# Attention and two MoE layers on one core: a deeper weight decode, tanh gates, and stacked fp32r scores

## The chip, the core and the metric

The kernel runs on one core of one Trainium2 chip. Its engines work side by side, each through its own queue in order: TensorE (PE, with its weight loads as PEld), VectorE (DVE), ScalarE (ACT), GpSimd (POOL), and SyncE (SP), which here only issues DMAs. The metric is the device time of one execution in microseconds. A profiled execution also has a span, from the first to the last recorded instruction; the times inside a profile count from the span's start.

## The reference

Attention over 4 batches, 8 heads, 576 positions and 64 dimensions keeps, in each row of scores, the 32 largest; then come two MoE layers with dense weights (512 to 1536 and back) over the 2304 tokens.

```python
scores = scale * np.matmul(q, k.transpose(0, 1, 3, 2))
kth = np.partition(scores, -top_k, axis=-1)[..., -top_k:-top_k + 1]
scores = np.where(scores >= kth, scores, -1000000000.0)
attn = np.exp(scores - np.max(scores, axis=-1, keepdims=True))
attn = attn / (np.sum(attn, axis=-1, keepdims=True) + 1e-09)
x = np.matmul(attn, v)                       # heads joined: (2304, 512)
g = x @ w_gate
x = (g * (1.0 / (1.0 + np.exp(-g))) * (x @ w_val)) @ w_out      # first MoE
gate = 1.0 / (1.0 + np.exp(-(x @ w2_gate)))
out = (gate * (x @ w2_val)) @ w2_out                            # second MoE
```

The weights come to the core as 64-bit floats and are turned into fp32 on it.

## The kernel before

The tokens are cut into six chunks of 4, 5, 6, 7, 7 and 7 query tiles of 64 tokens (`SIZES`). For each chunk `attention` computes x, head pair by head pair, and `moe` runs both MoE layers on it. A segment is the part of a chunk that lies in one batch, for one head pair.

Scores: `score_ops` multiplies a tile of 64 queries by 288 keys, one head at a time. Two query tiles and two heads are four matmuls on different quarters of the array (64 rows by 64 columns, fp32), which fill one PSUM tile `ps_s`; ACT copies it to `s` (`cp`). A row tile is 128 rows of 576 scores. `row_tile` finds its 32nd largest score on DVE with four MAX8 and three MATCH_REPLACE8 steps, ACT takes exp of all scores into `e`, and DVE masks and sums them in one operation (`mask`, L695). The reciprocal of the sum scales the row, `turned` transposes it on PE into `ps_t`, and `pv` multiplies it by V into `ps_v`.

Weights: a slab is 1024 columns of 128 rows; it has two half-slabs. Chunk 0 runs with plain fp32 weights (mode N), and `decode` makes them: a DMA brings a half-slab of 64-bit numbers (`wr`), ACT scales the high words to `wf`, the sign and the lower bits are brought to `wu`, and DVE merges both (L483). For the sign half of the half-slabs use ACT and POOL (`s1`, `s2`), the others DVE (`f2`, L457); this is `SP`. Each `wf` is used by chunk 0's MoE and also stored to memory (`sw`). The rings (the sets of buffers) hold 3 `wr` and 8 `wf`.

Chunks 1 to 5 (mode P) read `sw` back as `raw`, and `split_ops` cuts it into a high fp32r part (a copy on ACT or POOL, L434 and L436) and the rest (a subtraction on POOL or DVE, L439). x and the hidden rows are cut in the same way (`xh`, `xl`, `hh`, `hl`). A product is then three fp32r terms, 12 matmuls for one 512-deep contraction (`mms`, L805).

The gates: ACT computes silu in the first MoE and the sigmoid in the second (L834), and DVE multiplies by the other branch. These functions and exp need different tables on ACT, so changing between them costs an ACT_TABLE_LOAD.

Early scores: while chunk 0 runs, `early` computes the scores of three of chunk 5's four head pairs (`EARLY`) into memory (`se` to `ss`); chunk 5 loads them back.

The order of all this is not written out by hand. Each step is recorded by `op` with a duration, its inputs, its buffers and a priority (`P_QK`, `E_DMA` and so on; a lower number goes first), and `Plan.run` places the steps on the engines before anything is issued. Each engine then runs its list in order. The buffers of chunk 0's decode (phase 0) and those of the split weights (phase 1) share memory, so phase 1 cannot take its buffers before the last use of phase 0.

The lines of the profile that matter: L575 native scores, L695 the mask, L729 and L731 the top-32 steps, L762 transposes, L781 products with V, L805 MoE matmuls, L453 to L483 the decode, L434 to L439 the splits.

## Time and profile before

| | us |
|---|---|
| median of 3 runs | 1341.06 (1339.08 to 1344.63) |
| profiled execution | 1339.5 |
| its span | 1337.7 |
| PE busy in it | 1252.6 |
| DVE busy in it | 1105.1 |
| ACT busy in it | 911.2 |
| POOL busy in it | 775.2 |

Busy time is the time in which an engine had at least one instruction under way. The ends of matmuls are modelled, and matmuls follow each other like items on a belt, so the time for which one holds PE is read from its start to the start of the next, not from its own duration. DVE and POOL time includes waiting for one another inside an instruction. In rows with an idle time, the name behind the arrow is what ended it.

### The profile page before, as it was taken

How to read it: one execution, taken by the hardware profiler on the slowest of the kernel's cores; microseconds unless marked ns; L12 is line 12 of the kernel's file. 1: busy time of each engine (PE TensorE's matmuls, PEld its weight loads, DVE VectorE, ACT ScalarE, POOL GpSimd, SP SyncE). 2: the span in 40 equal slices, each digit the busy share in tenths (PEclk: the TensorE clock that was granted, in tenths of full speed). 3: DMA queues.
4: the chain of work that ended last, by engine and by line, in shares of the span. 5: the costliest groups of instructions: out<-in, count | busy, mean ns of one | idle time of the engine just before them, and what ended most of it. 6: DMA issues, size and time to landing. Idle time of an engine off the chain costs nothing.

```text
span 1337.7 us, 22187 instructions
## 1 busy us (share of the span) xinstructions
PE 1252.6 (94%) x7504; PEld 1030.6 (77%) x7504; DVE 1105.1 (83%) x2325; ACT 911.2 (68%) x1592; POOL 775.2 (58%) x841
## 2 busy tenths in 40 slices
PE   4478988887999999999999999999999999999998
PEld 1235666555888888888888887899888899999998
DVE  7994999998999999999999999999999455344442
ACT  6566878796997988986896877688678333332331
POOL 4101444433997987875887676699677445343431
PEclk9868999998999999999999999999999999999999
DMA  8245888886343444433334333444522223433231
GB/s 271 91 141 184 258 253 265 268 269 229 130 136 129 143 130 135 136 107 122 113 106 154 103 101 125 147 137 134 182 79 78 97 98 107 147 102 123 98 111 67
DMA packets 93426, 194.19 MB, mean 145 GB/s; under 512 B 10369, under 2 KB 17537, under 8 KB 93313
## 3 DMA queue, kind: packets, MB, share of 16 engines
q1 hardware_dynamic: 93312, 192.78, 44.1%
q8 instruction: 59, 0.97, 0.3%
q14 instruction: 55, 0.44, 0.1%
HBM read 162.96 MB, written 29.79 MB: 144 GB/s over the span
## 4 chain that ended last, share of the span: by engine, by line
PE 74%; ACT 7%; DMA 6%; DVE 4%; issue 1%; POOL 1%; SPq 0%; ACTq 0%; POOLq 0%; DVEq 0%
PE ps_m L805 59%; PE ps_v L781 5%; PE ps_s L575 5%; PE ps_t L762 5%; DMA wr<-in_wall_dram 3%; DVE st L729 1%; ACT L834 1%; DMA sw<-wf 1%; DVE wk L731 1%; DMA raw<-sw 1%; ACT wf L453 1%; ACT L687 1%; DVE p L695 1%; ACT e L687 1%; DMA ss<-se 1%
## 5 line engine op out<-in xcount | busy, mean ns | idle before, releaser
L439 POOL TENSOR_TENSOR w<-raw,w 128x512 fp32r<-128x512 f32 x297 | 404.9, 1372 | 23.2 <-ACT w L434 16.9
L805 PE MATMUL ps_m<-xh,w 128*128 128x448 f32 (+2 forms) x1920 | 403.2, 351 | 1.5 <-ACT sil L834 1.3
L805 PEld LDWEIGHTS ps_m<-xh,w 128*128 128x128 f32 x1920 | 334.9, 188 | 38.2 <-issue 13.9
L729 DVE MAX8 st<-wk 128x8 f32<-128x576 f32 x432 | 312.4, 745 | 0.1
L436 POOL TENSOR_SCALAR w<-raw 128x512 fp32r<-128x512 f32 x169 | 111.9, 666 | 246.8 <-PE ps_m L805 128.2
L434 ACT ACTIVATE w<-raw 128x512 fp32r<-128x512 f32 x191 | 119.7, 628 | 148.4 <-PE ps_m L805 117.3
L805 PE MATMUL ps_m<-xl,w 128*128 128x448 f32 (+2 forms) x960 | 216.0, 346 | 0.4 <-POOL xl L439 0.4
L731 DVE MATCH_REPLACE8 wk<-st,wk 128x576 f32<-128x576 f32 x288 | 212.4, 739 | 0.0
L805 PE MATMUL ps_m<-hh,w 128*128 128x448 f32 (+2 forms) x960 | 201.2, 351 | 0.0
L805 PEld LDWEIGHTS ps_m<-hh,w 128*128 128x128 f32 x960 | 167.7, 188 | 16.5 <-issue 7.6
L805 PEld LDWEIGHTS ps_m<-xl,w 128*128 128x128 f32 x960 | 172.1, 188 | 8.1 <-POOL xl L439 0.7
L695 DVE SCALAR_TENSOR_TENSOR p<-s,st,e 128x576 f32<-128x576 f32 x144 | 157.6, 1094 | 0.1
L575 PE MATMUL ps_s<-k,q 64*64 64x288 f32 x984 | 104.8, 462 | 34.4 <-ACT s L581 29.7
L439 DVE TENSOR_TENSOR w<-raw,w 128x512 fp32r<-128x512 f32 x63 | 70.3, 1118 | 79.8 <-POOL w L436 61.0
L762 PE MATMUL ps_t<-ident,p 128*128 128x128 f32 (+1 forms) x736 | 115.6, 287 | 14.6 <-ACT p L708 11.0
L762 PEld LDWEIGHTS ps_t<-ident,p 128*128 128x128 f32 (+1 forms) x736 | 87.8, 144 | 53.4 <-ACT p L708 18.7
L851 DVE TENSOR_TENSOR h<-sil,ps_m 128x448 f32<-128x448 f32 (+2 forms) x120 | 69.0, 575 | 72.1 <-PE ps_m L805 63.4
L768 ACT ACTIVATE pt<-ps_t 128x512 f32<-128x512 f32 (+3 forms) x256 | 105.6, 438 | 18.5 <-PE ps_t L762 17.4
L687 ACT ACTIVATE e<-s,st 128x576 f32<-128x576 f32 x144 | 111.6, 775 | 3.8 <-POOL st L683 1.8
L729 DVE MAX8 st<-s 128x8 f32<-128x576 f32 x144 | 106.7, 742 | 8.0 <-ACT s L581 8.0
L805 PE MATMUL ps_m<-hl,w 128*128 128x448 f32 (+2 forms) x480 | 107.9, 346 | 0.0
L731 DVE MATCH_REPLACE8 wk<-st,s 128x576 f32<-128x576 f32 x144 | 106.3, 739 | 0.0
(57 smaller groups left out, 1636.5 us busy)
## 6 DMA issues: line engine op xcount, KB each, us to landing
raw<-sw SPq DMA_DIRECT2D x360, 256.0 KB, 2.8
wr<-in_wall_dram SPq DMA_DIRECT2D x72, 512.0 KB, 4.8
sw<-wf SPq DMA_DIRECT2D x72, 256.0 KB, 5.2
v<-in_vL_dram SPq DMA_DIRECT2D x32, 320.0 KB, 3.0
...
```

Of the source, the lines that this page charges most:

```text
L434: nc.scalar.activation(out=hi(), in_=raw(), func=AF.Copy)
L436: nc.gpsimd.tensor_scalar(hi(), raw(), 1.0, 1.0, op0=ALU.mult, op1=ALU.mult)
L439: (nc.gpsimd if eng == "pool" else nc.vector).tensor_sub(lo(), (lo_raw or raw)(), lo_hi() if lo_hi else f32(hi()))
L575: nc.tensor.matmul(psg[y:y + 64, h, :288], qg[r, (o + j) * 64:(o + j + 1) * 64], kg[r, x * 288:x * 288 + 288], start=True, stop=True)
L687: nc.scalar.activation(out=eg[:], in_=src(), func=AF.Exp, bias=stg[:, 32:33], scale=SCALE)
L695: nc.vector.scalar_tensor_tensor(out=o, in0=src(), scalar=stg[:, 31:32], in1=eg[:], op0=ALU.is_ge, op1=ALU.mult, accum_out=stg[:, 33:34])
L729: nc.vector.max(out=stg[:, 4 * k:4 * k + 8], in_=src() if k == 0 else wk())
L731: nc.vector.match_replace(out=wk(), in_to_replace=stg[:, 4 * k - 4:4 * k + 4], in_values=src() if k == 1 else wk(), imm_value=NEG)
L762: nc.tensor.transpose(tg[:width, i], pg[:, a:a + width], ident)
L768: nc.scalar.activation(out=dst(), in_=src(), func=AF.Copy)
L805: nc.tensor.matmul(pg[:, :n], blk(a, d), src(x, d), start=first and i == 0, stop=last and i == 4 * len(terms) - 1)
L851: nc.vector.tensor_mul(h32[:, :n], sg[:, :n], pg[:, :n])
```

## The change

It has these parts.

1. The decode is deeper: 16 `wf` buffers for 8 and 4 `wr` buffers for 3 (`WF`, `WR`), and all half-slabs take their sign through ACT and POOL (`SP = 4`). The buffers of `w`, `q` and `k` now belong to one phase each.
2. Both gates are computed with tanh, in the table that exp uses: `sigmoid(x) = (1 + tanh(x/2))/2`. In the first MoE a DVE operation makes `(t + 1) * x` from it, one more for each gate tile, and the factor 1/2 moves into the copy of the MoE's result. The second MoE uses `(t + 1) * val` in the place of the product.
3. In chunk 0, row tiles are masked ahead of exp (`BEFORE`): DVE writes a large negative number where a score is under the 32nd (`cut`), POOL adds the scores, and ACT takes exp and the sum in one operation.
4. For head pairs 1 to 3 of chunk 2 and all of chunks 3 and 4, `stacked` loads each head's keys twice, one copy over the other (`kD`), and cuts them into `kh` and `kl`; it loads the queries twice too (`qD`), and writes the high part into partitions 0 to 63 and the rest into 64 to 127 of `qs`. `stacked_scores` multiplies `qs` by `kh` and by `kl`, with 128 rows and 128 columns, in fp32r.
5. All four head pairs of chunk 5 have early scores now, and these are recorded between the row tiles of chunks 0 and 1 (two and one for a pair of row tiles) and no longer in one piece behind chunk 0's attention; their DMAs have priority 5, it was 7.
6. Some durations that the planner uses are different.

```diff
+NAT = 2
+NATP = 1
-EARLY = "000003"
-E_FIRST = 64
+EARLY = "000004"
+E_FIRST = 0
+E_IN = [2, 1, 0, 0, 0, 0]
+BEFORE = [1, 0, 0, 0, 0, 0]
+WR = 4
-E_DMA = 7
-SP = 2
+E_DMA = 5
+SP = 4
-WF = 8
+WF = 16
+KS_RING = 1
+QS_RING = 1
...
+            specs.update(qr=([P, Q], F32, 1), qs=([P, Q], F32R, QS_RING), kr=([P, S], F32, KR_RING),
+                         kh=([P, S], F32R, 2 * KS_RING), kl=([P, S], F32R, 2 * KS_RING))
...
+    def stacked(bp, q0, n):
...
+        for h in range(2):
+            kr, kh, kl = new(("kr", ph)), new(("kh", ph)), new(("kl", ph))
+            ld = load(kr, kD[bp, :, h], n_bytes=P * S * 4, prio=1)
+            ops += split_ops(lambda kh=kh: kh[:], lambda kl=kl: kl[:], lambda kr=kr: kr[:], S, [kr], [ld], P_K, P_K,
+                             allocs=[kh, kl])
...
+        ops += split_ops(lambda: qs[:, :W], lambda: qs[up, :W], lambda: qr[:, :W], W, [qr], lds, P_K, P_K, allocs=[qs],
+                         lo_raw=lambda: qr[up, :W], lo_hi=lambda: f32(qs[up, :W]))
...
+    def stacked_scores(sg, kq, o, m):
...
+                for h in range(2):
+                    at = o * 64 + (h * n * 64 + h * 64 * (n % 2) if m == 2 else 0)
+                    for i in range(2):
+                        nc.tensor.matmul(psg[:, h, :288], qs[:, at:at + P], keys[h][i][:, x * 288:x * 288 + 288],
+                                         start=(i == 0), stop=(i == 1))
...
+        def cut():
+            take(eg)
+            nc.vector.tensor_scalar(eg[:], src(), stg[:, 31:32], NEG, op0=ALU.is_lt, op1=ALU.mult)
+
+        def add():
+            nc.gpsimd.tensor_tensor(out=eg[:], in0=eg[:], in1=src(), op=ALU.add)
+
+        def ex_sum():
+            take(pg)
+            nc.scalar.activation(out=pg[:, e * S:(e + 1) * S], in_=eg[:], func=AF.Exp, bias=stg[:, 32:33],
+                                 scale=SCALE, accum_out=stg[:, 33:34])
...
+    def gated(out, t, x):
+        nc.vector.scalar_tensor_tensor(out=out, in0=t, scalar=1.0, in1=x, op0=ALU.add, op1=ALU.mult)
...
-                                nc.scalar.activation(out=sg[:, :n], in_=pg[:, :n],
-                                                     func=AF.Silu if moe_i == 0 else AF.Sigmoid)
+                                nc.scalar.activation(out=sg[:, :n], in_=pg[:, :n], func=AF.Tanh, scale=0.5)
+                            if moe_i == 0:
+                                def silu(pg=pg, sg=sg, n=n):
+                                    gated(sg[:, :n], sg[:, :n], pg[:, :n])
+                                g_op = op("dve", dve(n), silu, deps=[g_op], uses=[pg, sg], prio=0)
```

How the planner's lists move is seen best at three places. The first is DVE at the end of chunk 0's attention: the last steps of chunk 0's last row tile and what stands behind them. Before (`st_912` is that row tile, `wf` the decode):

```order
L731 MATCH_REPLACE wk_926<-st_912,wk_926 128x576
L729 MAX st_912<-wk_926 128x8
L731 MATCH_REPLACE wk_926<-st_912,wk_926 128x576
L729 MAX st_912<-wk_926 128x8
L695 SCALAR_TENSOR_TENSOR p_931,st_912<-s_621,st_912,e_924 128x576
L699 TENSOR_SCALAR st_912<-st_912 128x1
L703 RECIPROCAL st_912<-st_912 128x1
L483 SCALAR_TENSOR_TENSOR wf_1027<-wf_1027,wu_296 128x512
L843 TENSOR_TENSOR hn_1045<-sil_1034,ps_m_1029 128x256
L483 SCALAR_TENSOR_TENSOR wf_1048<-wf_1048,wu_266 128x512
```

After (`st_1116` is chunk 0's last row tile, `st_1154` and `st_1202` are the first of chunk 1):

```order
L824 MAX st_1116<-wk_1128 128x8
L826 MATCH_REPLACE wk_1167<-st_1154,wk_1167 128x576
L765 TENSOR_SCALAR e_1193<-s_933,st_1116 128x576
L824 MAX st_1154<-wk_1167 128x8
L824 MAX st_1202<-s_1034 128x8
L826 MATCH_REPLACE wk_1167<-st_1154,wk_1167 128x576
L826 MATCH_REPLACE wk_1215<-st_1202,s_1034 128x576
L797 RECIPROCAL st_1116<-st_1116 128x1
L824 MAX st_1154<-wk_1167 128x8
L824 MAX st_1202<-wk_1215 128x8
L789 SCALAR_TENSOR_TENSOR p_1231,st_1154<-s_1034,st_1154,e_1195 128x576
```

The mask of the last row tile (L695) has become a cut (L765), and behind it stand the steps of chunk 1's rows, not the decode of the next half-slabs.

The second is SP at the change from phase 0 to phase 1: the last stores of decoded weights (`sw`), the output of chunk 0, and the first loads for chunk 1 (`raw`). Before:

```order
L487 DMA sw_96<-wf_2663 128x512
L487 DMA sw_96<-wf_2679 128x512
L487 DMA sw_97<-wf_2710 128x512
L487 DMA sw_97<-wf_2730 128x512
L561 DMA ss_2_6_164<-se_1020 128x1152
L902 DMA out_dram<-h_3_2775 128x256
L427 DMA k_2795<-in_kT_dram 128x576
L427 DMA q_2801<-in_qT_dram 128x384
L561 DMA ss_2_8_165<-se_1065 128x576
L427 DMA raw_2854<-sw_62 128x512
L427 DMA raw_2868<-sw_62 128x512
```

After:

```order
L503 DMA sw_96<-wf_2804 128x512
L1013 DMA out_dram<-h_2_2898 128x256
L503 DMA sw_97<-wf_2807 128x512
L503 DMA sw_97<-wf_2815 128x512
L443 DMA kr_2998<-in_kD_dram 128x576
L1013 DMA out_dram<-h_3_3010 128x256
L443 DMA kr_3026<-in_kD_dram 128x576
L597 DMA qr_3045<-in_qD_dram 128x384
L443 DMA raw_3051<-sw_62 128x512
L443 DMA raw_3055<-sw_62 128x512
L443 DMA raw_3062<-sw_63 128x512
L601 DMA qr_3045<-in_qD_dram 128x384
```

The early stores (`ss`) are gone from this place, and loads of keys and queries for chunk 2 (`kr`, `qr`) stand in front of the first `raw`.

The third is PE at the beginning of chunk 1's MoE (`xh`, `xl` and `w` are its operands; `ps_s` holds scores of chunk 2). Before:

```order
L805 MATMUL ps_m_2939<-xh_2856,w_2895 128x320 x8
L805 MATMUL ps_m_2939<-xl_2857,w_2895 128x320 x4
L575 MATMUL ps_s_2961<-k_2410,q_2421 64x288 x4
L805 MATMUL ps_m_2974<-xh_2856,w_2895 128x320 x8
L805 MATMUL ps_m_2974<-xl_2857,w_2895 128x320 x4
L762 MATMUL ps_t_2992<-ident,p_2897 128x128 x4
L762 MATMUL ps_t_3003<-ident,p_2897 128x128
L575 MATMUL ps_s_3005<-k_2410,q_2421 64x288 x4
L805 MATMUL ps_m_3016<-xh_2856,w_2905 128x320 x8
L805 MATMUL ps_m_3016<-xl_2857,w_2905 128x320 x4
L805 MATMUL ps_m_3039<-xh_2856,w_2905 128x320 x8
L805 MATMUL ps_m_3039<-xl_2857,w_2905 128x320 x4
```

After:

```order
L911 MATMUL ps_m_3099<-xh_3005,w_3069 128x320 x8
L911 MATMUL ps_m_3099<-xl_3006,w_3069 128x320 x4
L911 MATMUL ps_m_3129<-xh_3005,w_3069 128x320 x8
L911 MATMUL ps_m_3129<-xl_3006,w_3069 128x320 x4
L857 MATMUL ps_t_3151<-ident,p_3057 128x128 x4
L857 MATMUL ps_t_3160<-ident,p_3057 128x128
L622 MATMUL ps_s_3162<-kh_3048,qs_3096 128x288
L622 MATMUL ps_s_3162<-kl_3049,qs_3096 128x288
L622 MATMUL ps_s_3162<-kh_3059,qs_3096 128x288
L622 MATMUL ps_s_3162<-kl_3060,qs_3096 128x288
L911 MATMUL ps_m_3176<-xh_3005,w_3086 128x320 x8
L911 MATMUL ps_m_3176<-xl_3006,w_3086 128x320 x4
```

A group of four native score matmuls of 64 columns (L575) has become four single fp32r matmuls of 128 columns (L622) on the split keys and queries, in about the same places.

## Rows read from the trace of the kernel before

**Rows 1.** Page, part 1: busy us, share of the span, instructions.
```profile
PE 1252.6 (94%) x7504; PEld 1030.6 (77%) x7504; DVE 1105.1 (83%) x2325; ACT 911.2 (68%) x1592; POOL 775.2 (58%) x841
```
**Rows 2.** Windows, four stages: stretch, its length, then the columns of the heading.
```profile
core 0: us, PE busy (x) PEld busy (x) DVE busy (x) ACT busy (x) POOL busy (x), PEclk, DMA share, GB/s
0.00:116.20 116.20, 67.50 (x432) 28.36 (x432) 98.59 (x221) 68.41 (x127) 20.51 (x44) 0.82 0.48 164
116.20:321.60 205.40, 180.17 (x955) 129.71 (x952) 180.45 (x382) 162.68 (x283) 83.24 (x113) 0.98 0.83 259
321.60:333.20 11.60, 7.93 (x71) 3.86 (x70) 11.60 (x28) 9.18 (x21) 6.47 (x9) 1.00 0.47 159
333.20:1337.70 1004.50, 996.96 (x6055) 868.70 (x6053) 814.49 (x1696) 670.98 (x1162) 664.95 (x676) 1.00 0.36 120
```
**Rows 3.** Timeline around 116 us: start, length, engine, what, [idle before <-releaser].
```profile
106.86 0.16 DVE L703 RECIPROCAL st<-st 128x1 f32<-128x1 f32 x1
116.22 1.99 PE L805 MATMUL ps_m<-xn,wf 128*128 128x256 f32 x8
118.96 0.69 DVE L483 SCALAR_TENSOR_TENSOR wf<-wf,wu 128x512 int32<-128x512 int32 x1 [11.94 <-ACT wf L453]
```
**Rows 4.** Groups of DVE, 0 to 116.2 us: busy, mean ns | idle before.
```profile
L729 DVE MAX8 st<-wk 128x8 f32<-128x576 f32 x48 | 34.5, 741 | 0.1
...
L695 DVE SCALAR_TENSOR_TENSOR p<-s,st,e 128x576 f32<-128x576 f32 x16 | 12.9, 803 | 0.1
...
L483 DVE SCALAR_TENSOR_TENSOR wf<-wf,wu 128x512 int32<-128x512 int32 x8 | 6.5, 818 | 0.0
...
L457 DVE TENSOR_SCALAR wu<-wf 128x512 int32<-128x512 int32 x4 | 2.0, 507 | 0.1
```
**Rows 5.** Waits of PE, 116.2 to 321.6 us: total us, times, longest.
```profile
PE ps_m L805 <- DVE wf L483: 12.6, 9, 4.2
...
PE ps_m L805 <- ACT wf L453: 2.1, 1, 2.1
```
**Rows 6.** Groups of POOL, 333.2 to 1057.1 us.
```profile
L439 POOL TENSOR_TENSOR w<-raw,w 128x512 fp32r<-128x512 f32 x246 | 334.3, 1369 | 18.1 <-ACT w L434 14.0
...
L436 POOL TENSOR_SCALAR w<-raw 128x512 fp32r<-128x512 f32 x121 | 80.8, 673 | 93.9 <-PE ps_m L805 85.0 <-DMA raw<-sw 6.6 <-issue 1.2
```
**Rows 7.** Timeline of PE, three places: native scores among MoE matmuls, split MoE matmuls.
```profile
222.30 0.70 PE L575 MATMUL ps_s<-k,q 64*64 64x288 f32 x4
222.93 1.99 PE L805 MATMUL ps_m<-xn,wf 128*128 128x256 f32 x8
...
225.40 0.72 PE L575 MATMUL ps_s<-k,q 64*64 64x288 f32 x8
226.05 1.13 PE L805 MATMUL ps_m<-xn,wf 128*128 128x256 f32 x4
...
341.79 1.33 PE L805 MATMUL ps_m<-xh,w 128*128 128x320 f32 x8
342.96 0.75 PE L805 MATMUL ps_m<-xl,w 128*128 128x320 f32 x4
```
**Rows 8.** The chain of waits in chunk 3's MoE matmuls: start, us, what.
```profile
852.51 2.41 PE ps_m L805 x12
```
**Rows 9.** Groups of DVE, 333.2 to 1057.1 us.
```profile
L695 DVE SCALAR_TENSOR_TENSOR p<-s,st,e 128x576 f32<-128x576 f32 x107 | 126.2, 1179 | 0.0
...
L851 DVE TENSOR_TENSOR h<-sil,ps_m 128x448 f32<-128x448 f32 (+2 forms) x84 | 46.7, 556 | 18.6 <-PE ps_m L805 10.9 <-ACT sil L834 1.9 <-issue 1.7
```
**Rows 10.** Groups of ACT over the span: table loads ahead of gates.
```profile
L834 ACT ACT_TABLE_LOAD x70 | 89.8, 1283 | 1.1
```
**Rows 11.** Windows of other stretches, columns as in rows 2.
```profile
333.00:500.00 167.00, 164.13 (x1178) 139.09 (x1178) 161.87 (x371) 146.60 (x253) 149.34 (x151) 1.00 0.42 135
...
333.20:1057.10 723.90, 720.17 (x4676) 610.30 (x4674) 693.41 (x1557) 579.80 (x1009) 560.37 (x574) 1.00 0.38 125
1057.10:1337.70 280.60, 276.79 (x1382) 258.40 (x1380) 121.07 (x139) 91.18 (x153) 104.57 (x102) 1.00 0.31 106
```

More of the change, by code (lines that the diff above doesn't have):

```diff
@@ L52 @@
 P_QK = 2
+P_K = 1
 P_PT = 2
@@ L70 @@
 K_RING = 2
+KS_RING = 1
+QS_RING = 1
+KR_RING = 2
 V_RING = 2
@@ L342, in attn_moe_kernel @@
     scr32 = [drp.tile([P, 2, 512], F32, tag=f"sw{i}", name=f"sw{i}") for i in range(N_SLAB)]
-    scratch = [drp.tile([P, 2, 8, P], F32, tag=f"scr{i}", name=f"scr{i}") for i in range(N_SLAB if "R" in MODES else 0)]
+    scratch = [drp.tile([P, 2, 8, P], F32, tag=f"scr{i}", name=f"scr{i}") for i in range(N_SLAB if set(MODES) & set("Rab") else 0)]
     HW = max(n * 64 if n <= 8 else n * 32 for n in SIZES)
@@ L372, in attn_moe_kernel @@
         chunks.append((g * 64, n, segs))
-    kinds = [{"N": 0, "S": 1, "P": 1, "R": 1}[m] for m in MODES]
+    kinds = [{"N": 0}.get(m, 1) for m in MODES]
     PHASE = [sorted(set(kinds)).index(k) for k in kinds]
@@ L508, in slab @@
         mode, ph = MODES[c], PHASE[c]
+        mode = {"a": "PS", "b": "SR"}.get(mode, mode * 2)[i % 2]
         if mode == "N":
@@ L518, in slab @@
             return out
-        w = new("w")
+        w = new(("w", ph))
         def block(x):
@@ L657, in segment @@
                     done = score_ops(sg, [sg], kg, qg, lds, o, m, P_QK, P_S)
-                norms = [row_tile(sg, new("st"), done, e, pg) for e in range(m)]
+                norms = [row_tile(sg, new("st"), done, e, pg, BEFORE[c]) for e in range(m)]
+                tiles[0] += 1
+                if tiles[0] > E_SKIP:
+                    step(E_IN[c])
                 for k3 in range(3):
@@ L688, in ex @@
                                  bias=stg[:, 32:33], scale=SCALE)
-        m0 = op({"act": (180, P_EX), "pool": (200, P_EX)}, 0, neg, deps=[m0], uses=[stg])
-        x = op("act", act(S), ex, deps=[m0], uses=[sg, stg], allocs=[eg], prio=P_EX, table="exp")
+        if before:
+            x = op("dve", 380, cut, deps=[last], uses=[sg, stg], allocs=[eg], prio=P_MASK, lock=True)
+            x = op("pool", pool_tt(S), add, deps=[x], uses=[sg, eg], prio=P_CUT)
+            y = op("act", act(S), ex_sum, deps=[m0, x], uses=[eg, stg], allocs=[pg], prio=P_EX, table="exp")
+        else:
+            x = op("act", act(S), ex, deps=[m0], uses=[sg, stg], allocs=[eg], prio=P_EX, table="exp")
         def mask():
@@ L710, in norm @@
                 nc.gpsimd.tensor_scalar(o, o, stg[:, 35:36], 1.0, op0=ALU.mult, op1=ALU.mult)
-        y = op("dve", 729, mask, deps=[last, x], uses=[sg, stg, eg], allocs=[pg], prio=P_MASK, lock=True)
+        if not before:
+            y = op("dve", 729, mask, deps=[last, x], uses=[sg, stg, eg], allocs=[pg], prio=P_MASK, lock=True)
         y = op({"dve": (69, P_MASK), "pool": (200, P_MASK)}, 0, eps, deps=[y], uses=[stg])
@@ L788, in pv, with product @@
         return op("act", act_ps(W), cp, deps=[a], uses=[og], allocs=[x32g], prio=1)
+    def gated(out, t, x):
+        nc.vector.scalar_tensor_tensor(out=out, in0=t, scalar=1.0, in1=x, op0=ALU.add, op1=ALU.mult)
+    def product(out, gate, val, moe_i):
+        if moe_i == 0:
+            nc.vector.tensor_mul(out, gate, val)
+        else:
+            gated(out, gate, val)
     def moe(c):
@@ L807, in mms @@
                     i += 1
-        if c == 0:
+        if c == 0 and E_FIRST:
             step(E_FIRST)
```

130 lines of the change are left out of this document (88 added, 42 removed).

## The prediction, made before the changed kernel ran

> **What bounds the kernel now.** I read the table of engine loads first. PE is busy for 94% of the span, DVE for 83%, and no other engine comes near [rows 1]. That is an average over unlike stages, so next I cut the span where the program changes [rows 2]. From 333.2 us (the first matmul of chunk 1's MoE) to the end PE is busy 997.0 of 1004.5 us: there the end moves only if PE gets less to do or is made to wait. Before it lie three others. Up to 116.2 us (chunk 0's attention) DVE is the bound: from 8 us on it has no hole to speak of until the last reciprocal of chunk 0 at 106.86 us, and the first MoE matmul follows at 116.22 us [rows 3, 4]. From 116.2 to 321.6 us (chunk 0's MoE) PE is busy 180.2 of 205.4 us [rows 2]. The missing 25 us are waits, 14.7 of them for weights just decoded [rows 5]; behind those stands the load of the raw weights, with the DMA engines 83% busy [rows 2]. From 321.6 to 333.2 us the kernel changes its buffers, and nothing of chunk 1's MoE can start.
>
> The profiled execution took 1339.5 us, 1.8 us over its span and 1.6 us under the median of the runs (1341.06). I sum the change against the profiled execution and add the 1.6 us at the end.
>
> **Chunk 0's attention: 6 us later.** Up to chunk 0's last reciprocal the order of DVE holds, before, 64 maxima, 48 replacements, 16 masks, 8 decode merges and 4 sign operations. After, it holds 68, 52, 16 cuts, 16 merges and no sign operation. Added are 8 row steps of 0.74 us and 8 merges of 0.82 us [rows 4], 12.5 us. Gone are 4 sign operations of 0.51 us [rows 4] and, 16 times, the mask less the cut. The trace has no such cut. It lies between the sign operation stretched from 512 to 576 columns (0.57) and the mask it replaces (0.80) [rows 4]; I take 0.57, since both are tensor_scalars with one tensor as input, and save 3.7 us. That makes +6.8. The added row steps belong to chunk 1 and may only fill holes (0), and the detour over POOL, some 1.54 us for 576 columns by the row of POOL's 512-column subtraction [rows 6], may show in the last row tile (+10). I take +6. The 16 more groups of native scores that lie in this stage now are beside the DVE work: PE is busy 67.5 of 116.2 us there [rows 2].
>
> **Chunk 0's MoE: 19 us shorter.** PE's own work is 180.2 us [rows 2]. By the order the stage keeps its 288 matmuls, three products with V and its transposes, and has 25 groups of native scores in place of 32. One holds PE for 0.65 us (225.40 to 226.05) [rows 7], so 4.5 us go: 175.7. Now the waits. Before, DVE stands still for 11.9 us at the start of this stage, waiting for a decoded half-slab [rows 3], since only 8 were ready. With 16 buffers twice as many are, and by the order of SP 20 raw half-slabs are asked for ahead of the stage, where it was 11. That leaves 52 loads of 0.52 MB and 56 stores of 0.26 MB (128 x 1024 and 128 x 512 numbers of 4 bytes) where there were 61 and 64: some 46 MB in place of the 53 that 259 GB/s moved in 205.4 us [rows 2]. At the same rate that takes 178 us, as long as PE's work. Two near-bounds of one length don't fit perfectly, so I keep 10 us of waits, from 3 to 25. The stage takes 186 us.
>
> **The change of buffers: 11 us, before 11.6.** The early stores that stood last in SP's queue are gone from there, but POOL gets two key splits of 1.54 us in front of the first weight split [rows 6]. One takes about what the other gives; 8 to 14.
>
> **From chunk 1's MoE on: 12 us less work, 4 us of new waits.** Before, 87 groups of native scores lie here. A group is four matmuls of 64 by 64, and holds PE for only 0.65 us, as they run side by side; a group of two, for a single query tile, takes 0.63 us (222.30 to 222.93) [rows 7]. At 0.64 they make 55.7 us. After, there are 82 groups of four fp32r matmuls of 288 columns. The trace has none of 288; one of 320 takes 0.146 us (1.17 us for eight, 341.79 to 342.96) [rows 7] and one of 448 takes 0.201 us (2.41 us for 12) [rows 8], so by the line through both one of 288 takes 0.133 us, and 0.146 at the worst. 328 x 0.133 is 43.7 us: 12.0 us less (7.8 by the upper price). Nothing else of PE's work changes in this stage. New waits can come from the splits of keys and queries, and from the gates of the first MoE, where a DVE operation now stands between tanh and the release of the PSUM bank. I take 4 us for them, from 0 to 20.
>
> DVE's 60 new gate operations up to chunk 4 (0.56 us each, as the products they resemble [rows 9], 34 us) and ACT's lost table loads (those ahead of the gates alone are 70 and 89.8 us [rows 10]) lie off the path. The last product with V ends at 1057.1 us, and of the 280.6 us from there to the end [rows 11] chunk 5's MoE (864 x 0.201) needs only 174. In the new order 1128 MoE matmuls stand behind the last product with V, where 1380 did: this cover shrinks from 107 to some 53 us and is not used up, since DVE gets those 50 us too.
>
> The sum: +6, -19.4, -0.6, -12.0 and +4 make -22. 1339.5 - 22 is 1317.5, and 1319 on the median.
>
> **A rule that speaks against it.** DVE's masks take 0.80 us each while POOL is busy 18% of the time [rows 2, 4], and 1.18 us from 333 to 1057 us, where POOL is 77% busy [rows 9, 11]. The 38 key and 19 query splits, less the weight copies that move to ACT, put some 40 us on POOL's 560 in this stage; if the excess of 0.38 us grows with POOL's load, the 108 masks get 3 us longer in all, inside the 53 us of cover.
> The Trainium skill, SBUF — State Buffer, "Who interferes with whom", says that a DVE operation with two SBUF inputs and a GpSimd operation that reads SBUF contend for one set of ports, and that the second to issue waits for the whole of the first. The two means of this trace agree with it.
>
> **Rivals.** (a) *The decode stays as slow as it is.* If the DMA engines and not the buffers set the pace, chunk 0's MoE keeps its 205 us: 1319 + 19 = 1338, no measurable change. For it speaks the 83%; against it that the same engines are only 48% busy before 116 us [rows 2], and the deeper ring uses just that time. (b) *POOL becomes the bound of chunks 1 and 2.* By the order POOL's work for chunk 1's weights, keys and hidden rows (72 weight subtractions of 1.37, 24 of hidden rows of 0.86, 10 keys of 1.54 and smaller ones) is 157 us beside some 165 us of PE. If it also stands idle 18 us, as it does from 333 to 500 us today [rows 11], it needs 175: +10, and as much again in chunk 2 makes 1339. Against it: POOL spends 85 us of this stage waiting for PE to free a weight buffer [rows 6], so it runs ahead. (c) *Slower: every segment waits for its keys.* The split keys have one set of buffers, so the next segment's splits start only behind the last score matmul of the one before. In the order the tightest place has four groups of 12 matmuls at 1.76 us (12 x 0.146) and five transposes between them, 7.7 us of PE work. The chain is ACT's copy (0.78, by POOL's own copy of 512 columns [rows 6]), two keys of 1.54, a split of h of 0.86 and the queries at 2.06 us (768 columns): 6.8 us without any wait in POOL's queue. There are 18 such handovers. If two weight splits stand in front each time, PE waits 2 to 3 us: +36 to +54, so 1351 to 1369. It decides from 1.8 us a handover, where the kernel is at 1348. Against it: the same idle POOL, and gaps of 8 to 14 us at the later handovers. (d) *Better:* chunk 0's MoE keeps only 3 us of its waits, no new ones come, and the attention of chunk 0 takes no longer: 1319 - 7 - 4 - 6, about 1302.
>
> **Chances.** Forecast 0.60, (d) 0.12, (a) 0.11, (b) 0.08, (c) 0.09. About 0.5% (6.7 us) is what a measurement of this kernel can tell: faster is under 1334.4, slower over 1347.8. The forecast and (d) are faster, with a little of (a) and (b): 0.77. No change 0.14, slower 0.09. The forecast's own range is 1304 to 1333. The other cases widen it to 1298 to 1339, which leaves out (c) and the ends of the others.
>
> **What would show it.** Right: the first MoE matmul at about 122 us, the last of chunk 0 near 308, the first of chunk 1 near 319, the waits for decoded weights halved, one table load in all, groups of four score matmuls at 0.53 us, and PE without holes from there on. Wrong: score groups that wait for kl or qs by 2 us each (c), weight matmuls of chunks 1 and 2 that wait for POOL (b), or chunk 0's MoE ending after 325 us with the DMA engines still over 80% busy (a).

## The result, and the profile after

The changed kernel takes 1303.06 us (median of 4 runs, 1300.36 to 1303.84), the one before 1340.32 beside it: a ratio of 0.9713 [0.9686, 0.9739]. That is 37 us faster, and 16 us better than the 1319 forecast. Its profiled execution took 1302.69 us with a span of 1300.9. All medians here leave out one execution of 3105.84 us, the profiled one of the run with the old rings, whose profile is not used for that reason.

The page's busy times of the changed kernel, which answer to [rows 1]:

```profile
PE 1241.8 (95%) x7240; PEld 1062.6 (82%) x7240; DVE 1110.6 (85%) x2345; ACT 837.5 (64%) x1662; POOL 862.7 (66%) x853
```

PE has 11 us less to do, ACT 74 less, POOL 88 more, DVE 6 more. The four stages, cut at the same events as [rows 2]:

```profile
0.00:131.17 131.17, 86.78 (x549) 33.73 (x549) 113.72 (x242) 95.83 (x190) 60.88 (x82) 0.79 0.65 226
131.17:300.84 169.67, 166.34 (x908) 127.21 (x905) 160.24 (x341) 140.32 (x271) 88.29 (x120) 1.00 0.81 267
300.84:309.92 9.08, 4.98 (x35) 3.71 (x33) 9.08 (x21) 6.53 (x14) 8.23 (x8) 0.95 0.79 260
309.92:1300.90 990.98, 983.70 (x5758) 897.94 (x5756) 827.53 (x1745) 594.87 (x1189) 705.33 (x644) 1.00 0.41 130
```

Chunk 0's attention became 15.0 us longer, chunk 0's MoE 35.7 us shorter, the change of buffers 2.5 shorter, and all that follows 13.5 shorter: 36.8 in all. In chunk 0's MoE PE is now busy 166.3 of 169.7 us, where it was 180.2 of 205.4. Its waits there, of which [rows 5] shows 14.7 us for decoded weights before, are these, and none is for a decoded weight:

```profile
PE ps_s L639 <- ACT s L656: 1.2, 1, 1.2
PE ps_s L639 <- ACT s L649: 1.0, 3, 0.6
PE ps_t L857 <- ACT p L802: 0.6, 1, 0.6
...
```

The place that [rows 3] showed, in the timeline of the changed kernel (L797 is the reciprocal, L911 the MoE matmul; the next rows of the same engine stand between them):

```profile
123.65 0.16 DVE L797 RECIPROCAL st<-st 128x1 f32<-128x1 f32 x1
123.73 1.40 DVE L824 MAX8 st<-wk 128x8 f32<-128x576 f32 x2
125.05 0.80 DVE L789 SCALAR_TENSOR_TENSOR p<-s,st,e 128x576 f32<-128x576 f32 x1
...
131.17 1.99 PE L911 MATMUL ps_m<-xn,wf 128*128 128x256 f32 x8
```

Before, DVE stood still for 11.9 us here. Now it goes on with the rows of chunk 1, without a hole.

The stacked scores, in PE's timeline at the beginning of chunk 1's MoE; [rows 7] has the native ones:

```profile
316.87 0.75 PE L911 MATMUL ps_m<-xl,w 128*128 128x320 f32 x4
317.45 0.29 PE L622 MATMUL ps_s<-kh,qs 128*128 128x288 f32 x1
317.59 0.30 PE L622 MATMUL ps_s<-kl,qs 128*128 128x288 f32 x1
317.72 0.29 PE L622 MATMUL ps_s<-kh,qs 128*128 128x288 f32 x1
317.86 0.29 PE L622 MATMUL ps_s<-kl,qs 128*128 128x288 f32 x1
317.99 1.19 PE L911 MATMUL ps_m<-xh,w 128*128 128x320 f32 x7
```

From start to start one takes 0.135 us, and the four hold PE for 0.54 us: the forecast had 0.133 and 0.53.

**The account that the prediction did not make.** DVE's groups up to the first matmul of chunk 1's MoE, of the kernel before (0 to 333.2 us):

```profile
L729 DVE MAX8 st<-wk 128x8 f32<-128x576 f32 x115 | 83.8, 745 | 0.1
L731 DVE MATCH_REPLACE8 wk<-st,wk 128x576 f32<-128x576 f32 x76 | 56.1, 738 | 0.0
L483 DVE SCALAR_TENSOR_TENSOR wf<-wf,wu 128x512 int32<-128x512 int32 x72 | 53.2, 745 | 21.1 <-ACT wf L453 13.9 <-POOL wu L480 5.0 <-ACT wu L478 1.3
...
L457 DVE TENSOR_SCALAR wu<-wf 128x512 int32<-128x512 int32 x36 | 16.6, 461 | 7.2 <-ACT wf L453 7.0
```

and of the changed one (0 to 309.92 us):

```profile
L824 DVE MAX8 st<-wk 128x8 f32<-128x576 f32 x115 | 83.6, 746 | 0.0
L499 DVE SCALAR_TENSOR_TENSOR wf<-wf,wu 128x512 int32<-128x512 int32 x72 | 57.1, 805 | 7.6 <-POOL wu L496 2.9 <-issue 1.9 <-POOL st L760 1.0
L826 DVE MATCH_REPLACE8 wk<-st,wk 128x576 f32<-128x576 f32 x76 | 56.2, 740 | 0.0
```

The counts are the same: when chunk 1's MoE can begin, DVE has done the same maxima, replacements and merges in both kernels. The time of that moment is DVE's work up to it and the time in which DVE does nothing: 290.6 + 42.6 = 333.2 us before, 283.0 + 26.9 = 309.9 after. So of the 23.3 us gained up to there DVE's holes make up 15.7. The waits in front of merges and sign operations, 28.3 us, are now 7.6, in front of merges only. The other 7.6 us are work: the 36 sign operations (16.6 us) are gone and 16 cuts took the place of masks, against 12 new gate operations (4.9 us) and merges that take 0.805 us for 0.745.

This is an account and not yet a cause: it would add up for any engine. What came last at that moment is seen in the timeline:

```profile
306.72 0.86 POOL L455 TENSOR_TENSOR xl<-x,xh 128x320 fp32r<-128x320 f32 x1
307.22 1.22 ACT L450 ACTIVATE w<-raw 128x512 fp32r<-128x512 f32 x2 [1.15 <-DMA raw<-sw]
309.15 1.11 PE L857 MATMUL ps_t<-ident,p 128*128 128x128 f32 x4 [4.07 <-ACT p L802]
309.92 2.48 PE L911 MATMUL ps_m<-xh,w 128*128 128x320 f32 x8
```

The last part of chunk 1's x, which needs DVE's rows, is ready at 307.6 us. The first raw weights are asked for at 302.75 us, behind the store of chunk 0's last output, and ACT waits for them until 307.22; the copy `p` for the transposes that stand ahead in PE's queue comes behind them on ACT. So in the changed kernel the chain goes over the end of chunk 0's MoE and the weight loads, with DVE's rows ready just before. DVE has to keep up for this, and the runs below show what happens where it doesn't.

### The profile page after: what moved, and what is told of

Its sections match the earlier page's. It is cut to its first block, busy times and chain, and to the rows that moved or that the text cites. A ratio compares the mean times of both kernels' runs of the same rounds, so it can differ in the third digit from the quotient of the medians.

```text
span 1300.9 us, 21941 instructions
## 1 busy us (share of the span) xinstructions
PE 1241.8 (95%) x7240; PEld 1062.6 (82%) x7240; DVE 1110.6 (85%) x2345; ACT 837.5 (64%) x1662; POOL 862.7 (66%) x853
## 4 chain that ended last, share of the span: by engine, by line
PE 73%; DVE 9%; ACT 7%; DMA 4%; POOL 4%; issue 2%; SPq 0%; ACTq 0%; POOLq 0%; DVEq 0%
PE ps_m L911 58%; PE ps_t L857 5%; PE ps_v L876 5%; DVE st L824 3%; DMA wr<-in_wall_dram 3%; DVE wk L826 3%; PE ps_s L639 3%; PE ps_s L622 2%; DVE p L789 2%; DMA raw<-sw 1%; ACT wf L469 1%; ACT wg L484 1%; ACT s L649 1%; POOL w L455 1%; POOL wu L488 1%
## 5 line engine op out<-in xcount | busy, mean ns | idle before, releaser
L455 POOL TENSOR_TENSOR w<-raw,w 128x512 fp32r<-128x512 f32 x309 | 419.5, 1368 | 41.2 <-ACT w L450 31.9
L911 PE MATMUL ps_m<-xh,w 128*128 128x448 f32 (+2 forms) x1920 | 405.2, 353 | 0.4 <-POOL w L455 0.4
L911 PEld LDWEIGHTS ps_m<-xh,w 128*128 128x128 f32 x1920 | 337.5, 189 | 20.5 <-issue 1.5
L450 ACT ACTIVATE w<-raw 128x512 fp32r<-128x512 f32 x263 | 163.6, 628 | 172.4 <-PE ps_m L911 122.1
L911 PE MATMUL ps_m<-xl,w 128*128 128x448 f32 (+2 forms) x960 | 218.5, 349 | 0.0
L911 PE MATMUL ps_m<-hh,w 128*128 128x448 f32 (+2 forms) x960 | 201.7, 352 | 0.0
L452 POOL TENSOR_SCALAR w<-raw 128x512 fp32r<-128x512 f32 x97 | 64.1, 661 | 176.4 <-DMA raw<-sw 87.2
L911 PEld LDWEIGHTS ps_m<-xl,w 128*128 128x128 f32 x960 | 172.6, 188 | 9.7
L911 PEld LDWEIGHTS ps_m<-hh,w 128*128 128x128 f32 x960 | 168.6, 188 | 10.1 <-issue 0.9
L789 DVE SCALAR_TENSOR_TENSOR p<-s,st,e 128x576 f32<-128x576 f32 x128 | 145.3, 1135 | 0.0
L857 PE MATMUL ps_t<-ident,p 128*128 128x128 f32 (+1 forms) x736 | 116.2, 288 | 12.0 <-ACT p L802 9.0
L940 ACT ACTIVATE sil<-ps_m 128x448 f32<-128x448 f32 (+3 forms) x144 | 70.1, 487 | 70.5 <-PE ps_m L911 69.5
L455 DVE TENSOR_TENSOR w<-raw,w 128x512 fp32r<-128x512 f32 x51 | 53.9, 1058 | 65.5 <-POOL w L452 45.6
L911 PE MATMUL ps_m<-hl,w 128*128 128x448 f32 (+2 forms) x480 | 109.3, 349 | 0.0
L802 ACT ACTIVATE p<-p,st 128x576 f32<-128x576 f32 x116 | 89.4, 771 | 22.2 <-DVE st L797 21.5
L777 ACT ACTIVATE e<-s,st 128x576 f32<-128x576 f32 x128 | 99.1, 774 | 3.1 <-POOL st L760 1.3
```

The lines of the kernel that those rows point to most:

```text
L450: nc.scalar.activation(out=hi(), in_=raw(), func=AF.Copy)
L455: (nc.gpsimd if eng == "pool" else nc.vector).tensor_sub(lo(), (lo_raw or raw)(), lo_hi() if lo_hi else f32(hi()))
L777: nc.scalar.activation(out=eg[:], in_=src(), func=AF.Exp, bias=stg[:, 32:33], scale=SCALE)
L789: nc.vector.scalar_tensor_tensor(out=o, in0=src(), scalar=stg[:, 31:32], in1=eg[:], op0=ALU.is_ge, op1=ALU.mult, accum_out=stg[:, 33:34])
L802: nc.scalar.activation(out=o, in_=o, func=AF.Copy, scale=stg[:, 35:36])
L857: nc.tensor.transpose(tg[:width, i], pg[:, a:a + width], ident)
```

## The experiments

The theory after the result was that two things bring the gain. The deeper ring and the lost table loads free chunk 0's MoE together (Theory A), and the stacked scores give what follows (Theory B). The rival was that one part alone does it, or that the order of the early scores does. The kernels ran on several chips, so each is given by its ratio to the kernel before on the same chip; differences between two ratios are turned into us with 1340. With every edit the planner orders the steps anew, so what a run gives is the worth of a part together with that order. Lines of `...` mark where an edit is cut.

**One part taken out of the changed kernel.** The first takes the rings back to their old depth:

```diff
-WR = 4
+WR = 3
-WF = 16
+WF = 8
```

> The changed kernel with the decode's old rings: 8 buffers of decoded half-slabs for 16 and 3 of raw ones for 4; all else as changed. Theory A (the ring freed chunk 0's MoE): the stage goes from 169.5 us back to 190 to 205 us, with waits of PE for decoded weights of over 10 us, and the kernel to 1320 to 1335. Rival C (ACT's lost table loads freed it): the stage stays under 180 us and the kernel at 1300 to 1310.

Measured: 1319.22 us, 0.9838 [0.9821, 0.9854], just under the range of Theory A and above that of Rival C. The depth is worth 17 us. For want of a profile it isn't shown where these 17 us lie, and the stage that the theory named is not measured.

The second computes all scores natively:

```diff
-NAT = 2
+NAT = 99
...
```

> The changed kernel with native fp32 scores in all chunks: no stacked keys and queries, no splits of them on POOL and ACT. Theory B (the stacked groups save PE 0.1 us each): the stage from chunk 1's MoE on has 79 groups of 0.64 us (50.6) for 82 of 0.53 (43.8), so it grows from 991 to 998 us, and the kernel goes to 1309 to 1312. Rival (the splits cost as much as the matmuls save): 1300 to 1305, with the named waits of PE for POOL and ACT falling by as much.

Measured: 1312.77 us, 0.9779 [0.9762, 0.9796]. The stages up to chunk 1's MoE end at 312.3 us, 2.4 later, and from there it takes 1000.4 us for 991.0. So the stacked scores give 9.4 us in the stage where they lie. PE's work there is 995.6 us for 983.7, and PE is idle 4.9 us for 7.3: the stacked scores save 11.9 us of work and bring 2.4 us of waits.

The third brings silu and sigmoid back, and so the table loads:

```diff
-nc.scalar.activation(out=sg[:, :n], in_=pg[:, :n], func=AF.Tanh, scale=0.5)
+nc.scalar.activation(out=sg[:, :n], in_=pg[:, :n], func=AF.Silu if moe_i == 0 else AF.Sigmoid)
...
-table="exp"
+table="silu" if moe_i == 0 else "sigmoid"
...
```

> The changed kernel with silu and sigmoid from their own tables again (no DVE operation between gate and release, no factor 1/2). Theory A: the stage of chunk 0's MoE grows by less than 8 us, and the kernel stays at 1300 to 1312, since ACT is off the path. Rival C: with some 20 table loads of 1.28 us back in that stage it goes to 190 us or more, and the kernel to 1322 to 1335.

Measured: 1352.8 us, 1.0087 [1.0068, 1.0106]. That is above the range of both theories: this one part takes away the whole gain and 12 us more. Its table loads over the span, in the groups of ACT, and the waits of PE in its chunk 0's MoE (132 to 342 us):

```profile
L940 ACT ACT_TABLE_LOAD x63 | 80.8, 1283 | 2.2 <-PE ps_m L911 1.3
L777 ACT ACT_TABLE_LOAD x59 | 75.7, 1283 | 1.0
```
```profile
PE ps_m L911 <- ACT sil L940: 13.7, 6, 5.7
PE ps_s L639 <- ACT s L649: 4.4, 4, 1.9
PE ps_s L639 <- ACT se L656: 3.6, 1, 3.6
PE ps_t L857 <- ACT p L802: 2.6, 2, 1.7
```

Only 22 of these loads, 28 us of ACT, lie in chunk 0's MoE, but it takes 209.9 us for 169.7. From chunk 1's MoE on it takes 14.8 us more.

The fourth masks chunk 0 behind exp, as before:

```diff
-BEFORE = [1, 0, 0, 0, 0, 0]
+BEFORE = [0, 0, 0, 0, 0, 0]
```

> The changed kernel with chunk 0's rows masked behind exp, as before (no cut on DVE, no addition on POOL). Theory D (the way DVE, POOL, ACT and back leaves holes on DVE, 8.9 us of named waits after the first 8 us and more inside instructions): the first MoE matmul comes at 118 to 122 us for 131.2, and the kernel at 1291 to 1297. Rival (the holes come from decoding 16 half-slabs beside the rows): DVE gets 16 x 0.2 us more, the first MoE matmul stays at 131 or later, and the kernel at 1303 to 1308.

Measured: 1299.75 us, 0.9688 [0.9672, 0.9703]. Chunk 0's MoE begins 7.0 us earlier and ends at 300.9, as it did: the earlier start is lost again. The early mask is worth nothing, or costs 3 us. Theory D was right in that the detour leaves holes, but the kernel stays above its 1291 to 1297.

**One part put into the kernel before.** First the tanh gates alone:

```diff
-    func=AF.Silu if moe_i == 0 else AF.Sigmoid)
+    func=AF.Tanh, scale=0.5)
...
```

> The kernel before with the tanh gates alone (rings, scores, masks, early scores as before). Theory C (the table switches held up chunk 0's MoE): the stage falls from 205 to 185 us or less and the kernel to 1300 to 1320. Theory A (the ring is what counts, the tables only hurt together with it): the kernel stays at 1330 to 1342, since PE's waits there are for decoded weights and 8 buffers remain.

Measured: 1336.91 us, 0.9966 [0.9942, 0.999]: 4.6 us, and chunk 0's MoE takes 209.4 us for 205.4.

Then the deeper decode alone:

```diff
-SP = 2
+SP = 4
-WF = 8
+WF = 16
-wr=([P, 512, 2], I32, 3)
+wr=([P, 512, 2], I32, 4)
...
```

> The kernel before with the deeper decode alone: 16 and 4 buffers, all signs through ACT and POOL, w in the second phase. Theory A: chunk 0's MoE falls to 190 us or less, the kernel to 1318 to 1328. Theory C (as long as the tables switch, ACT cannot feed the ring, and the sign path puts more on it): 1338 to 1355.

Measured: 1351.51 us, 1.0073 [1.0044, 1.0102]. Chunk 0's MoE falls to 194.2 us, but begins 13.5 us later, and from chunk 1's MoE on it takes 1021.2 us for 1004.5. So alone the gates give 4.6 us and the deeper decode costs 10, while taking the gates out of the changed kernel costs 50 and taking the depth out 17. The two edits of the decode are not the same, since here the signs move to ACT and POOL with it (`SP`), and there they stayed. The parts work only together, or with a third thing.

**The plan or the loads?** The tanh gates stay on the chip, but the planner believes that they need other tables:

```diff
-op("act", act_ps(n), ev, deps=[m], uses=[pg], allocs=[sg], prio=0, table="exp")
+op("act", act_ps(n), ev, deps=[m], uses=[pg], allocs=[sg], prio=0, table="silu" if moe_i == 0 else "sigmoid")
```

> The changed kernel with tanh on the chip, but planned as if silu and sigmoid still had tables of their own: the planner holds gates and exps back into bunches and reckons with loads that the chip then does not make. Theory C1 (the order that switching forces is what costs, gates held back while PE waits): 1335 to 1350, PE's waits for sil in chunk 0's MoE stay over 8 us. Theory C2 (the 22 loads of 1.28 us in that stage, and the rest later, are what costs): 1303 to 1315.

Measured: 1326.44 us, 0.987 [0.984, 0.99], between the two theories. So 21 of the 50 us are the order that the planner chooses when it counts loads, and the other 29 the loads themselves and the gates as they were.

**The early scores.** They go back to three pairs in one piece behind chunk 0's attention:

```diff
-EARLY = "000004"
-E_FIRST = 0
-E_LAST = 1
-E_IN = [2, 1, 0, 0, 0, 0]
-E_DMA = 5
+EARLY = "000003"
+E_FIRST = 64
+E_LAST = 0
+E_IN = [0, 0, 0, 0, 0, 0]
+E_DMA = 7
```

> The changed kernel with the early scores as before: three head pairs, recorded in one piece behind chunk 0's attention, DMA priority 7. Theory: the early groups are off the path while DVE is the bound, and the fourth pair moves 8 groups (4.3 us stacked) back into the PE-bound stage: 1305 to 1312. Rival (the early scores cost holes on DVE in chunk 0's attention, by ACT's copies): the first MoE matmul comes at 122 us or earlier, and the kernel at 1295 to 1302.

Measured: 1424.7 us, 1.06 [1.0569, 1.063], which no theory expected. PE's longest waits over its span are for ACT's copies of scores and for scaled rows, and the timeline shows what ACT waits for:

```profile
PE ps_s L639 <- ACT s L649: 54.0, 29, 6.5
PE ps_t L857 <- ACT p L802: 34.4, 15, 8.8
```
```profile
288.94 7.64 SPq L578 DMA_DIRECT2D ss<-se  x3
293.27 0.82 ACT L656 ACTIVATE se<-ps_s 64x288 f32<-64x288 f32 x2 [9.37 <-DMA ss<-se]
```

The last three stores of early scores stand behind all stores of decoded weights in SP's queue. The copy of the last early scores waits for a buffer that they free, and the copies of chunk 1's scores follow only from 297.59 us. So no row of chunk 1 is ranked while chunk 0's MoE runs (DVE is busy 54.4 of its 157.9 us), and 145.8 us lie between its end and chunk 1's MoE.

Is it the one piece, or that its DMAs stand at level 7, behind those of the decoded weights? The same kernel with one line different:

```diff
-E_DMA = 7
+E_DMA = 5
```

> As the run with the early scores in one piece, which took 1425 us, but with the DMAs of those early steps at the fifth level of the plan instead of the seventh. Theory (the early steps' loads stood behind the weight loads in the plan, and the ring of score buffers behind them): the kernel comes back to 1303 to 1315. Rival (the one piece itself blocks the ring of score buffers): it stays over 1380.

Measured: 1327.93 us, 0.9876 [0.9853, 0.9899]: between the two. The level of the DMAs made 97 of the 119 us; the last store of early scores now goes out at 139.51 us. So it was the stores that stood behind the weights, and not, as the theory had it, the loads. The one piece itself, with three pairs for four, still costs 22. Chunk 0's MoE begins 6.4 us earlier, and the loss lies at one place, in the change of buffers. These are its windows:

```profile
124.79:295.22 170.43, 165.22 (x886) 124.25 (x882) 144.25 (x301) 133.32 (x255) 89.75 (x117) 0.99 0.83 270
295.22:336.05 40.83, 22.54 (x136) 13.84 (x136) 40.83 (x97) 26.06 (x56) 16.84 (x18) 0.71 0.34 109
336.05:1327.00 990.95, 984.48 (x5778) 899.22 (x5776) 823.94 (x1724) 594.28 (x1192) 708.31 (x656) 1.00 0.41 128
```

Chunk 0's MoE is as short as in the changed kernel, and everything from chunk 1's MoE on takes the same 991 us. But between them lie 40.8 us for 9.1, and DVE is busy in all of them.

**The three together.** The kernel before with the gates, the deeper decode and the level of the DMAs:

```diff
-E_DMA = 7
-SP = 2
-WF = 8
+E_DMA = 5
+SP = 4
+WF = 16
...
-    func=AF.Silu if moe_i == 0 else AF.Sigmoid)
+    func=AF.Tanh, scale=0.5)
...
```

> The kernel before with three of the parts put in together: the tanh gates, the deeper decode (rings of 16 and 4, both stages in the first phase) and the plan's fifth level for DMA; the scores stay native, the mask stays behind the exponential, and the early scores of a chunk stay as three pairs in one piece. Alone the gates gave 4 us and the deeper decode lost 10. Theory (the two hold each other back, and together they carry all but what the stacked scores give): chunk 0's MoE falls from 205 to 170 to 180 us, the later stages stay near 1000, and the kernel takes 1310 to 1322. Rival (the interleaved early scores are needed for it too): it stays at 1336 to 1350.

Measured: 1338.89 us, 0.9958 [0.9941, 0.9975]. The stage came out about as the theory said (169.0 us), the kernel as the rival said. Its windows, then DVE's groups in the second of them and DVE's longest waits before it ends:

```profile
123.53:292.48 168.95, 168.76 (x934) 126.43 (x931) 151.87 (x317) 131.80 (x256) 99.01 (x131) 1.00 0.82 271
292.48:327.67 35.19, 17.38 (x115) 8.93 (x112) 33.27 (x78) 21.02 (x43) 18.35 (x24) 0.68 0.45 152
```
```profile
L729 DVE MAX8 st<-wk 128x8 f32<-128x576 f32 x18 | 13.0, 749 | 0.0
L731 DVE MATCH_REPLACE8 wk<-st,wk 128x576 f32<-128x576 f32 x12 | 8.9, 743 | 0.0
L695 DVE SCALAR_TENSOR_TENSOR p<-s,st,e 128x576 f32<-128x576 f32 x6 | 5.0, 837 | 0.0
```
```profile
DVE sil L791 <- ACT sil L843: 15.7, 6, 11.1
DVE st L729 <- ACT s L581: 8.0, 1, 8.0
DVE wf L483 <- POOL wu L480: 7.0, 12, 1.1
```

36 us were won in chunk 0's MoE, 7 lost ahead of it, and 24 came back at once, because PE was done and DVE was not: the rows of chunk 1 were still to be ranked. Here it is x that comes last: POOL splits the first weights from 301.70 us on, and x's last part is copied at 325.38. DVE had lost its time around the beginning of that MoE (it starts at 123.53 us), in one hole of 11.1 us up to 125.98, the same place where it stood 11.9 us before [rows 3]. With the early scores in one piece, no row of chunk 1 is there yet; DVE's next item is a gate of chunk 0, and it has to wait for PE.

**Is chunk 0's MoE held by PE or by the DMA engines?** Each decoded half-slab is stored a second time, to memory that nobody reads:

```diff
+        def again():
+            nc.sync.dma_start(twice[i][:, x], f[:])
+        op("dma", dma(128 * 2048), again, deps=[b], uses=[f], prio=6, lat=DMA_LAT)
```

> The changed kernel with each decoded half slab stored twice, the second time to memory that nobody reads: some 19 MB more of DMA writes, all of them in chunk 0's MoE. Theory A (TensorE sets the pace of that stage, busy 166 of its 170 us, and the DMA engines at 0.81 have room or give way): the kernel takes under 13 us more, 1303 to 1318. Theory B (the transfers of the weights and slabs set it): the stage grows by 45 to 60 us, and the kernel takes 1350 to 1370.

Measured: 1353.45 us, 1.0082 [1.0047, 1.0117], 49 us more than the changed kernel. The stage grew by 28 us, not by the 45 to 60 of Theory B; another 17 are in the change of buffers. Its windows, the longest wait of PE in the second of them, and SP's queue there (`tw` is the second store):

```profile
131.49:329.49 198.00, 179.03 (x958) 133.34 (x954) 184.04 (x403) 151.53 (x291) 92.30 (x132) 0.98 0.86 272
329.49:355.36 25.87, 4.79 (x26) 2.09 (x26) 2.98 (x5) 3.69 (x10) 3.16 (x3) 0.64 0.90 317
```
```profile
PE ps_m L916 <- ACT w L451: 20.9, 1, 20.9
```
```profile
346.27 0.60 SPq L504 DMA_DIRECT2D sw<-wf  x1
346.92 0.64 SPq L517 DMA_DIRECT2D tw<-wf  x1
347.61 1.32 SPq L444 DMA_DIRECT2D kr<-in_kD_dram  x2
348.97 0.48 SPq L602 DMA_DIRECT2D qr<-in_qD_dram  x1
350.89 0.80 SPq L444 DMA_DIRECT2D raw<-sw  x2
```

The first loads for chunk 1 (`kr`, `raw`) stand in SP's queue behind the last stores, and PE waits for them. In the stage the transfers ran at 272 GB/s, hardly above the 267 of the changed kernel. 19 MB at that rate are some 70 us, of which 49 showed, so by this estimate some 20 us of transfers found room beside the others. Other places for the stores were not tried. The kernel's time is in Theory B's range, the stage's growth is between the theories: PE's work and the transfers are both close to the length of the stage.

**One step further.** The ring of decoded weights at 20, with chunk 0's mask behind exp:

```diff
-BEFORE = [1, 0, 0, 0, 0, 0]
+BEFORE = [0, 0, 0, 0, 0, 0]
-WF = 16
+WF = 20
```

> The run with the mask behind the exponential, and the ring of decoded weights at 20 instead of 16. The changed kernel and that run began chunk 0's MoE at 131 and 124 us and ended it at the same 300.9. Theory A (the pace of the decode still sets that end, and a deeper ring moves it): the stage ends at 293 to 297 us and the kernel takes 1291 to 1297. Theory B (TensorE's own work sets it, with the clock and order it has): it ends near 301 again, and the kernel takes 1298 to 1302.

Measured: 1299.25 us, 0.9664 [0.9642, 0.9685]. The stage ends at 298.1, between the two theories, and the kernel's time is Theory B's. It is the fastest of all, 7 us by the ratios and 4 by the medians under the changed kernel, but the intervals don't tell it apart from the run with the mask behind exp and the ring at 16.

The account of DVE for all kernels with a profile (us; "idle" is the time to chunk 1's first MoE matmul less DVE's busy time):

| kernel | chunk 0's MoE | chunk 1's MoE begins | DVE busy to there | DVE idle | from there on |
|---|---|---|---|---|---|
| before | 205.4 | 333.2 | 290.6 | 42.6 | 1004.5 |
| before, tanh gates | 209.4 | 330.6 | 293.4 | 37.2 | 1004.7 |
| before, deeper decode | 194.2 | 330.9 | 286.0 | 44.9 | 1021.2 |
| before, both and DMA level | 169.0 | 327.7 | 288.9 | 38.7 | 1006.7 |
| after | 169.7 | 309.9 | 283.0 | 26.9 | 991.0 |
| after, early scores in one piece | 170.4 | 336.1 | 287.0 | 49.1 | 991.0 |
| after, the same with the DMAs at level 7 | 157.9 | 429.3 | 284.4 | 144.9 | 992.9 |
| after, native scores | 174.3 | 312.3 | 279.7 | 32.5 | 1000.4 |
| after, silu and sigmoid | 209.9 | 348.6 | 305.3 | 43.4 | 1005.8 |
| after, plan with tables | 191.5 | 330.3 | 300.3 | 30.1 | 994.7 |
| after, mask behind exp | 176.7 | 308.6 | 283.5 | 25.0 | 989.6 |
| after, the same with ring 20 | 173.1 | 306.0 | 284.7 | 21.3 | 989.9 |
| after, stores twice | 198.0 | 355.4 | 304.8 | 50.6 | 993.8 |

The first two numbers hardly follow each other: four kernels have a MoE of 169 to 173 us and begin chunk 1's between 306 and 336. The second is by its making the sum of the next two. What the table adds is that DVE's work up to there is nearly the same in most kernels, 280 to 293 us, so that they differ by its holes. Where it is 300 or more, more row steps had been put ahead of that point (643 instructions of DVE for 601 in the run with the plan changed). The table alone can't tell whether DVE held chunk 1's MoE or stood idle because something else did. With the stores twice it is the weight loads (20.9 us), in the runs with the three parts and with the one piece DVE's rows, and in the changed kernel the loads, with the rows close by.

## Why the prediction was right, and where it was off

The direction and the range held, and of the mechanism this: the decode was chunk 0's MoE's wait, and it is gone. But the prediction gave all of that to the deeper ring. Alone, the deeper decode shortens the stage by 11 us and loses 10 over all; it needs the tanh gates, and then the early scores between the row tiles, to keep what it wins. Neither had a gain in the sum. That all of these came in one change is the luck in this forecast: without the gates the kernel takes 1352.8 us, and with the early scores in one piece 1327.93. The size was 16 us short, by these terms.

- *Chunk 0's attention, +6 forecast, +15.0 measured.* The added steps and merges came as counted: up to chunk 0's last reciprocal DVE is busy 106.4 us for 98.6, 7.8 more where 6.8 was forecast. But that reciprocal comes at 123.65 us for 106.86, so 9 us are holes. The upper end was +10, with the detour of the mask over POOL showing once; it shows several times: DVE waited 3.9 us for the small addition on POOL behind the sum and 1.9 for ACT's exp, and besides 2.9 for POOL's part of the decode, none of which it did before. In the run with the mask behind exp the MoE begins 7.0 us earlier. The cut was priced at 0.57 us; it took 9.4 us for 16, 0.595. The rows of chunk 1 that lie in this stage are no loss: they are work that is done early.
- *Chunk 0's MoE, 186 forecast, 169.7 measured.* This is the mis-sized term. The waits were put at 10 us and are 3.3 (169.67 less 166.34), near the lower end given. The hole of 11.9 us that the prediction puts at the start of this stage runs from 107.0 to 119.0 us, so most of it lies ahead of the stage. PE's work was put at 175.7 and is 166.3: its 288 MoE matmuls (two records each) keep PE busy for 133.2 us, for 141.4 before. Part of the 180.2 us from which I started was low clock behind waits: after a wait of 4.20 us the clock granted from 315.0 to 321.6 us was 0.56, near the lower of its two levels (1.2 GHz of 2.4), and from 217.0 to 222.3 us, behind a wait of 2.09 us, it was 0.68. Eight matmuls took 6.56 and 5.38 us there, for 3.62 in the changed kernel. That is 4.7 of the 8.2 us; the rest isn't assigned. The rate of the transfers was sized well: 46 MB at 259 GB/s forecast, 267 GB/s for 169.7 us (45 MB) measured. The run with double stores shows that the transfers are a near-bound too: they make the stage 28 us longer.
- *The change of buffers, 11 forecast, 9.1 measured.* The number was right and its reason was not. I weighed two items in queues against each other. With a MoE of 169 to 170 us ahead of it, this stage is short only if the rows of chunk 1 are ranked by then, and for that the early scores lie between the row tiles: with the one piece it is 35 to 41 us. In the kernel before the one piece did no harm, as its MoE left 205 us for those rows. The prediction gave part 5 of the change no term of its own.
- *From chunk 1's MoE on, -8 forecast, -13.5 measured.* PE's work fell by 13.3 us (996.96 to 983.70), where 12.0 was forecast. Of the 4 us of new waits 2.4 came, by the run with native scores; they don't show against the kernel before, where PE was idle 7.5 us of it and is now 7.3. That run gives 9.4 us to the stacked scores.
- *"ACT's lost table loads lie off the path"* was the step that was wrong. It was true of the kernel before, from whose trace it was read: without the loads alone that kernel gains only 4.6 us. It isn't true of the changed kernel. With silu and sigmoid in its chunk 0's MoE, where ACT also makes the high words of every half-slab, PE waits 13.7 us for gates (4.3 before), and in all that follows the loads and gates cost 14.8 us (1005.8 for 991.0). Taken out of the changed kernel, the tanh gates are worth 50 us, more than the whole gain. The Trainium skill, ScalarE: Activation LUTs, "Table sets: the hidden batching unit", puts exp and tanh in one set and asks to batch by set. The trace agrees with the first: one load in all, where there are 123 with silu and sigmoid. The Trainium skill counts about 2.7 us for a change of set there; its section "What ACT_TABLE_LOAD costs" on the same page puts 1283 ns of it down to the load and the rest to a drain. Here each load is 1.283 us as well, but no drain shows: in the run with silu and sigmoid one runs from 207.60 us to 208.88, and the gate behind it starts at 208.90. The price of the change of tables can't be read from that time: 122 loads are 157 us of an engine that is busy 64% without them, the kernel loses 50, and 21 of these went with the order alone.

Of the rivals, (a) did not occur. The deeper decode alone comes nearest to it (1.0073, with a stage of 194.2 us); with the gates the ratio is 0.9958, but by another way, since the stage falls to 169.0 us and the time goes into the change of buffers. (b) and (c) did not occur: up to 1030 us the key splits took 1.57 us each on POOL (1.54 forecast), PE waited 0.4 us for POOL's weights and 0.3 for queries. (d), 1302, is where the kernel landed, by part of its reasons: 3 us of waits and hardly any new ones, but a longer attention of chunk 0. The masks took 1.188 us for 1.179 while POOL's share rose from 77 to 83% (up to 1057 us before and 1030 now): 1 us in all, where the rule that spoke against the change allowed 3.

What stays open: why the deeper decode alone makes the stages from chunk 1 on 17 us longer (the waits that PE shows there are 7.4 us, 5.5 of them for silu); where the 17 us of the ring's depth lie; and which of the early scores' settings (more pairs, no delay, between the tiles) gives how much of the 22 us. No run took out the new way of the signs or the planner's new durations by itself, or put the early scores alone into the kernel before. That DVE's rows hold the beginning of chunk 1's MoE is seen in the timelines of the runs with the one piece; in the changed kernel the weight loads came last, and no run made DVE's work alone longer or shorter to tell by how much.
